# First-layer products beside attention values issued as four column tiles, with new instruction orders, in a fused attention and MLP kernel

## The chip, the cores and the metric

The kernel runs on one NeuronCore of a Trainium2 chip. The metric is the device time of one execution in microseconds, given as the median of three runs. A profiled execution is a separate run of the same program.

## The reference

Causal attention with 16 "beacon" keys in front, followed by an MLP with a GELU in its sigmoid form. Eight batches, eight heads, 576 positions, head size 64; the MLP takes 4,608 tokens from 512 to 2,048 features and back.

```python
k_all = np.concatenate([beacon_k, k], axis=2)
v_all = np.concatenate([beacon_v, v], axis=2)
scores = scale * np.matmul(q, k_all.transpose(0, 1, 3, 2))
scores = np.where(causal, -1000000000.0, scores)      # the beacons are never masked
a = np.exp(scores - scores.max(-1, keepdims=True))
a /= a.sum(-1, keepdims=True) + 1e-09
x = np.matmul(a, v_all)            # then (B, H, S, D) -> (B*S, H*D)
h = x @ w_in
g = h * (1.0 / (1.0 + np.exp(-1.702 * h)))
out = g @ w_out                    # float32, 4608 x 512
```

## The kernel before

The attention works on 16 sets; set s is batch s // 2 and four of the eight heads. Keys and queries are loaded and cast to 16 bit by DMAs that POOL issues (L362), turned by VectorE (`e_turn`, L418), and multiplied in chunks of at most 512 score columns for each head (`e_qk`, L447). There are 55 chunks, named here scores 0 to 54. A score product contracts over 32 rows, and the four heads stand in four row tiles of the array (32\*128). ScalarE takes the exponential (`e_exp`, L458) into a buffer E, POOL masks the blocks on the diagonal (`e_mask`, L479; for the first two sets VectorE masks some), and `e_av` (L534) multiplies by the values: for each head 32 columns of V, so that four heads stand in four column tiles (128\*32) and write four parts of one PSUM bank. The same operation with a matrix of ones gives the sums for the division; VectorE turns and inverts these (L546 to L557) and normalises the values into xT (`e_norm`, L569). From set 4 on (batch 2), the sum of a set comes from a tile zs that VectorE adds up (L497).

The MLP follows in ten groups of tokens, two of 256 and eight of 512. The first layer has 16 steps a group when the group is 512 tokens wide (`e_m1`, L593): each is four matmuls of 128\*128 over 512 columns into one PSUM bank. xT holds four batches, 2,304 tokens, as a ring; where a group wraps around its end, a step is eight matmuls of 256. In groups 0 and 1, ScalarE computes a tanh and VectorE finishes the gate (L607, L626); in groups 2 to 9 ScalarE computes the GELU itself (`e_gelu`, L614). The exponential and this GELU are in different tables of ScalarE, and each change is an ACT_TABLE_LOAD. The second layer is a plain product in groups 0 and 1 (`e_m2`, L638) and a Strassen-Winograd form in groups 2 to 9 (`e_prod`, L707, seven products of 128\*128 tiles over 256 columns, with sums of operands made by VectorE, L658, and results joined by VectorE, L723). Stores go out on SyncE's queue.

Values, first-layer steps and second-layer products share four PSUM banks (tiles u0 to u3, `RING = 4`); the scores have the other four as one buffer, so the next scores wait for the exponential of the last. A bank comes free when the operation that closes it has read it: the GELU for a first-layer step, normalisation or inversion for values, a join for a product.

Loads through POOL are followed on eight DMA lanes: a POOL load waits until the eighth load before it has landed, and whatever stands behind it in POOL's order waits too. POOL is an in-order queue of loads and masks.

The order of work on each engine is written out by hand as lists of operation numbers, `ORDER`, one for each of PE, ACT, DVE, POOL, Q (the landing of a load) and SP. `Plan.run` walks these lists, works out a start time for each operation from costs and latencies (`LAT`), chooses a PSUM bank for each step by these times, and emits the operations sorted by start. It therefore doesn't change the order on an engine. The plan charges 114 ns where PE's `mode` changes between "m" (128\*128), "r" (row tiles) and "c" (column tiles). Names of operations below: `m1.g.n` is step n of group g's first layer, `m2.g.p.n` a part of product p of group g (for groups 0 and 1: row block p, quarter n), `av s.x.h` the values (x = 0 or 1) or sums (x = 2) of set s in half h.

Of the kernel before, what the change touches and what calls it, by code (L numbers as in the profile page):

```python
# [17 lines left out]
        76, 100, 115, 118, 120, 106, 138, 141, 143, 108, 155, 111, 152, 129, 161, 158, 122, 131, 164, 167, 134, 127,  # L18
        170, 173, 176, 145, 125, 148, 150, 177, 182, 188, 191, 227, 194, 197, 232, 183, 203, 234, 200, 178, 237,
        179, 206, 258, 241, 209, 184, 263, 185, 212, 265, 213, 248, 246, 268, 214, 215, 401, 251, 253, 272, 218,  # L20
        404, 275, 244, 279, 219, 220, 407, 282, 284, 277, 221, 414, 320, 296, 304, 290, 302, 292, 300, 298, 312,
        308, 294, 318, 314, 310, 306, 316, 426, 435, 423, 343, 338, 339, 340, 433, 431, 438, 344, 345, 359, 349,
        341, 464, 346, 350, 351, 352, 354, 574, 355, 429, 360, 361, 577, 356, 362, 357, 372, 365, 583, 474, 477,
        373, 366, 374, 367, 605, 480, 484, 375, 482, 607, 368, 506, 502, 488, 492, 610, 490, 486, 498, 504, 500,
        508, 514, 510, 516, 494, 496, 512, 534, 593, 596, 535, 536, 539, 540, 550, 541, 542, 537, 742, 545, 546,
        547, 548, 603, 745, 551, 552, 553, 599, 601, 619, 622, 748, 555, 556, 557, 558, 561, 755, 625, 627, 629,
        562, 563, 776, 568, 564, 569, 570, 571, 779, 764, 767, 659, 637, 641, 657, 649, 651, 647, 661, 635, 631,
        653, 805, 772, 770, 774, 643, 655, 633, 639, 645, 679, 680, 815, 818, 700, 681, 682, 684, 701, 915, 690,
        685, 686, 691, 692, 702, 918, 687, 693, 695, 703, 696, 924, 821, 823, 697, 698, 706, 946, 825, 707, 713,
        708, 709, 948, 934, 937, 714, 715, 716, 827, 951, 944, 940, 942, 853, 831, 833, 855, 857, 851, 843, 835,  # L30
        837, 847, 839, 845, 829, 849, 841, 1083, 960, 963, 875, 876, 880, 877, 878, 881, 882, 1086, 968, 966, 970,
        883, 1089, 902, 909, 903, 886, 891, 1096, 887, 888, 889, 892, 893, 1117, 904, 894, 905, 896, 897, 1120, 898,
        899, 910, 911, 1105, 1108, 1146, 912, 976, 994, 996, 972, 978, 1000, 992, 982, 974, 998, 990, 984, 988, 980,
        1002, 986, 1256, 1156, 1113, 1111, 1115, 1159, 1025, 1020, 1026, 1021, 1259, 1022, 1027, 1031, 1023, 1028,
        1265, 1164, 1162, 1166, 1041, 1042, 1287, 1036, 1047, 1032, 1048, 1033, 1037, 1038, 1034, 1039, 1289, 1054,
        1055, 1049, 1056, 1043, 1044, 1050, 1292, 1057, 1198, 1172, 1168, 1178, 1184, 1180, 1194, 1170, 1174, 1176,
        1275, 1278, 1182, 1186, 1196, 1188, 1190, 1281, 1301, 1285, 1283, 1304, 1216, 1217, 1221, 1192, 1222, 1227,
        1218, 1223, 1228, 1219, 1224, 1232, 1229, 1233, 1230, 1307, 1311, 1309, 1237, 1327, 1333, 1238, 1243, 1234,
        1244, 1235, 1323, 1239, 1245, 1250, 1251, 1341, 1240, 1246, 1252, 1253, 1337, 1405, 1315, 1331, 1343, 1411,
        1335, 1321, 1403, 1431, 1313, 1325, 1407, 1419, 1317, 1423, 1425, 1319, 1339, 1421, 1409, 1329, 1361, 1413,  # L40
        1366, 1382, 1429, 1362, 1363, 1401, 1367, 1364, 1427, 1368, 1383, 1372, 1369, 1373, 1374, 1375, 1388, 1377,
        1389, 1378, 1390, 1395, 1379, 1384, 1380, 1385, 1391, 1396, 1415, 1397, 1398, 1470, 1454, 1417, 1455, 1449,
        1471, 1450, 1451, 1476, 1452, 1456, 1477, 1457, 1478, 1460, 1461, 1462, 1463, 1465, 1466, 1467, 1468, 1472,
        1479, 1473, 1483, 1484, 1485, 1486,
# [3 lines left out]
        195, 198, 233, 235, 201, 204, 238, 180, 207, 259, 210, 264, 186, 266, 269, 216, 402, 405, 408, 222, 417,  # L48
        415, 297, 291, 303, 305, 301, 299, 293, 309, 321, 295, 319, 313, 315, 311, 307, 317, 436, 439, 342, 465,
        468, 575, 578, 584, 587, 606, 608, 503, 507, 489, 491, 493, 487, 499, 505, 509, 515, 517, 495, 501, 511,  # L50
        497, 513, 611, 538, 743, 746, 749, 756, 758, 777, 780, 660, 642, 638, 652, 658, 648, 650, 636, 632, 662,
        654, 806, 644, 634, 656, 640, 646, 809, 916, 683, 919, 928, 925, 947, 949, 952, 828, 832, 854, 856, 852,
        858, 834, 838, 844, 840, 836, 846, 830, 848, 850, 842, 1084, 879, 1087, 1090, 1099, 1097, 1118, 1121, 1147,
        1150, 977, 995, 979, 997, 993, 973, 975, 983, 991, 999, 989, 1001, 981, 1003, 985, 987, 1257, 1260, 1024,
        1269, 1266, 1288, 1290, 1293, 1199, 1179, 1173, 1181, 1185, 1195, 1171, 1169, 1175, 1177, 1183, 1187, 1197,
        1189, 1191, 1193, 1220, 1328, 1334, 1324, 1342, 1316, 1332, 1344, 1406, 1412, 1338, 1336, 1404, 1432, 1314,
        1408, 1420, 1318, 1424, 1326, 1426, 1320, 1340, 1422, 1410, 1330, 1322, 1414, 1430, 1402, 1365, 1428, 1416,
        1418, 1453,
# [3 lines left out]
        123, 163, 160, 124, 224, 169, 128, 166, 172, 175, 146, 147, 126, 149, 151, 225, 226, 398, 190, 193, 196,  # L62
        199, 255, 256, 257, 202, 205, 286, 242, 411, 287, 211, 208, 243, 399, 249, 247, 400, 250, 412, 254, 252,
        273, 245, 274, 280, 276, 413, 281, 285, 283, 278, 289, 461, 288, 462, 419, 580, 420, 463, 326, 327, 328,
        421, 322, 92, 323, 324, 422, 427, 428, 424, 425, 325, 330, 334, 329, 335, 432, 336, 331, 434, 337, 332, 333,
        470, 347, 582, 353, 471, 581, 472, 430, 473, 358, 363, 475, 476, 478, 479, 481, 485, 739, 483, 369, 376,
        370, 589, 752, 740, 590, 615, 518, 753, 921, 519, 754, 526, 591, 527, 520, 528, 592, 529, 521, 741, 522,
        597, 523, 594, 530, 595, 598, 531, 802, 532, 524, 533, 616, 543, 525, 604, 549, 617, 618, 554, 600, 620,
        602, 623, 624, 621, 559, 760, 628, 761, 762, 626, 630, 565, 763, 566, 768, 572, 765, 811, 812, 766, 803,
        804, 769, 773, 771, 671, 1080, 775, 672, 813, 922, 663, 814, 664, 675, 667, 816, 673, 819, 668, 669, 817,  # L70
        923, 665, 666, 820, 674, 676, 677, 1093, 670, 688, 694, 678, 930, 822, 824, 699, 931, 826, 932, 933, 704,
        710, 938, 939, 935, 936, 717, 711, 945, 941, 943, 1081, 956, 957, 958, 871, 1082, 1094, 1095, 959, 872, 873,
        867, 859, 961, 962, 964, 965, 860, 863, 1262, 1143, 861, 874, 862, 868, 864, 967, 865, 971, 866, 969, 884,
        869, 870, 1101, 1144, 890, 1145, 1102, 895, 1103, 1104, 900, 906, 1109, 907, 1110, 913, 1106, 1107, 1152,
        1153, 1004, 1154, 1005, 1155, 1264, 1006, 1263, 1016, 1012, 1017, 1157, 1114, 1112, 1013, 1018, 1116, 1160,
        1008, 1161, 1009, 1019, 1158, 1014, 1015, 1029, 1010, 1165, 1011, 1007, 1163, 1167, 1035, 1040, 1271, 1051,
        1045, 1058, 1052, 1297, 1272, 1273, 1274, 1298, 1299, 1276, 1279, 1300, 1200, 1204, 1280, 1201, 1277, 1205,
        1282, 1302, 1206, 1286, 1284, 1208, 1305, 1209, 1202, 1303, 1210, 1212, 1203, 1306, 1207, 1213, 1225, 1231,
        1308, 1312, 1214, 1310, 1215, 1211, 1236, 1247, 1241, 1248, 1254, 1349, 1345, 1350, 1346, 1347, 1353, 1351,
        1354, 1355, 1356, 1357, 1358, 1359, 1370, 1348, 1360, 1352, 1376, 1381, 1386, 1392, 1393, 1445, 1446, 1433,  # L80
        1399, 1437, 1434, 1438, 1447, 1435, 1441, 1442, 1436, 1443, 1444, 1439, 1448, 1440, 1458, 1464, 1469, 1480,
        1474, 1481, 1487,
    ],
    "POOL": [
        8, 10, 12, 14, 16, 17, 19, 21, 23, 25, 27, 29, 31, 33, 35, 37, 39, 41, 43, 45, 47, 110, 49, 51, 113, 114,
        53, 55, 57, 59, 133, 61, 136, 137, 63, 65, 67, 69, 71, 378, 230, 231, 229, 380, 382, 384, 386, 236, 388,
# [29 lines left out]

class Plan:

    LANES = 8
    LAT = {"PE": 230, "ACT": 178, "DVE": 212, "POOL": 110, "Q": 1400, "SP": 0}

    def __init__(self, ring):
        self.ops = []
        self.ring = ring
        self.tiles = {}
        self.closers = {}
# [1004 lines left out]
```

## Time and profile before

| | |
|---|---|
| median of 3 runs | 329.88 us (329.2 to 330.05) |
| profiled execution | 328.92 us, span 327.2 us |
| granted TensorE clock, mean | 0.999 |
| TensorE (PE) busy | 314.6 us, 4,364 matmul records |
| VectorE (DVE) busy | 237.2 us |
| ScalarE (ACT) busy | 202.1 us |
| GpSimd (POOL) busy | 113.9 us |

| group of instructions | count | busy us | mean ns of one |
|---|---|---|---|
| L593 PE, first layer, 128 x 512 and 128 x 256 | 704 | 130.6 | 341 |
| L707 PE, second layer, 128 x 256 | 896 | 121.0 | 273 |
| L447 PE, scores, 20 shapes | 1376 | 34.6 | 228 |
| L534 PE, values from E and V | 928 | 27.4 | 262 |
| L614 ACT, GELU | 128 | 70.5 | 598 |
| L458 ACT, exponentials | 66 | 98.9 | 1515 |

The span runs from the first to the last instruction; the device time has what lies around it as well. Busy time is the union of an engine's instructions. Matmuls are pipelined: the length of one is longer than the distance to the next one, so rates are read from starts. Matmuls in different tiles of the array overlap, and four of them start within some 10 ns. "Idle before" and "<-" name the time an engine stood still ahead of a row, and what ended it.

### The profile page before, as it was taken

How to read it: one execution, taken by the hardware profiler on the slowest of the kernel's cores; microseconds unless marked ns; L12 is line 12 of the kernel's file. 1: busy time of each engine (PE TensorE's matmuls, PEld its weight loads, DVE VectorE, ACT ScalarE, POOL GpSimd, SP SyncE). 2: the span in 40 equal slices, each digit the busy share in tenths (PEclk: the TensorE clock that was granted, in tenths of full speed). 3: DMA queues.
4: the chain of work that ended last, by engine and by line, in shares of the span. 5: the costliest groups of instructions: out<-in, count | busy, mean ns of one | idle time of the engine just before them, and what ended most of it. 6: DMA issues, size and time to landing. Idle time of an engine off the chain costs nothing.

```text
span 327.2 us, 9966 instructions
## 1 busy us (share of the span) xinstructions
PE 314.6 (96%) x4364; PEld 214.7 (66%) x4364; DVE 237.2 (72%) x480; ACT 202.1 (62%) x236; POOL 113.9 (35%) x178
## 2 busy tenths in 40 slices
PE   6589999999999999999999999999999999999995
PEld 6467665545775477746878878547764776447884
DVE  4838798777987989977998798858558853006674
ACT  1676697678767586679666786868577212674010
POOL 8765478190419312941177019400042000000000
PEclk9999999999999999999999999999999999999999
DMA  7999999293424911792039709500120012000122
GB/s 126 159 201 211 204 186 184 37 123 107 99 72 64 190 34 34 79 198 43 7 53 178 119 4 124 154 2 3 34 98 0 2 34 83 15 0 2 65 98 97
DMA packets 58220, 28.83 MB, mean 88 GB/s; under 512 B 41280, under 2 KB 53568, under 8 KB 58176
## 3 DMA queue, kind: packets, MB, share of 16 engines
q0 software_dynamic: 47552, 18.49, 47.9%
q1 hardware_dynamic: 10560, 9.69, 9.2%
q8 instruction: 34, 0.56, 0.7%
q14 instruction: 10, 0.08, 0.1%
q10 hardware_dynamic: 64, 0.01, 0.0%
HBM read 37.22 MB, written 9.44 MB: 143 GB/s over the span
## 4 chain that ended last, share of the span: by engine, by line
PE 83%; DMA 6%; DVE 4%; POOL 3%; ACT 2%; issue 1%; ACTq 0%; POOLq 0%
PE u L593 34%; PE u L707 30%; PE u L534 9%; PE s L447 7%; PE u L638 3%; DMA w<-in_moe_w_out_dram 3%; DMA w<-in_moe_w_in_dram 3%; ACT E L458 1%; DVE sA L658 1%; DVE g L626 1%; POOL vb L378 1%; POOL w L384 0%; DVE bkn L403 0%; ACT L614 0%; DVE kT L418 0%
## 5 line engine op out<-in xcount | busy, mean ns | idle before, releaser
L593 PE MATMUL u<-xT,w 128*128 128x512 f16 (+1 forms) x704 | 130.6, 341 | 0.6 <-ACT g L614 0.5
L458 ACT ACTIVATE E<-s 128x2048 f16<-128x2048 f32 (+5 forms) x66 | 98.9, 1515 | 44.9 <-PE s L447 44.4
L614 ACT ACTIVATE g<-u 128x512 f16<-128x512 f32 x128 | 70.5, 598 | 53.7 <-PE u L593 53.2
L593 PEld LDWEIGHTS <-w 128*128 128x128 f16 x704 | 67.6, 98 | 54.3 <-issue 1.9
L479 POOL TENSOR_SCALAR_AFFINE_SELECT E<-E 128x512 f16<-128x512 f16 (+3 forms) x78 | 49.3, 665 | 110.8 <-ACT E L458 79.1
L723 DVE SCALAR_TENSOR_TENSOR osb<-u,osb 128x512 f32<-128x512 f32 x56 | 37.3, 683 | 24.5 <-PE u L707 22.5
L707 PEld LDWEIGHTS <-g 128*128 128x128 f16 x512 | 48.3, 98 | 9.3 <-issue 0.2
L707 PE MATMUL u<-w,g 128*128 128x256 f16 x384 | 50.6, 273 | 0.0
L447 PE MATMUL s<-qT,kT 32*128 32x32 f16 (+20 forms) x1376 | 34.6, 228 | 5.7 <-ACT E L458 2.8
L447 PEld LDWEIGHTS <-kT 32*128 32x128 f16 x1376 | 25.2, 92 | 22.5 <-issue 14.4
L707 PEld LDWEIGHTS <-sA 128*128 128x128 f16 x384 | 36.3, 98 | 5.3 <-issue 0.3
L707 PE MATMUL u<-tB,sA 128*128 128x256 f16 x256 | 35.1, 273 | 0.1
L658 DVE TENSOR_TENSOR sA<-g 128x512 f16<-128x512 f16 x32 | 12.9, 416 | 26.2 <-ACT g L614 26.2
L569 DVE TENSOR_TENSOR xT<-u,rz 128x352 f16<-128x352 f32 (+2 forms) x52 | 25.5, 517 | 6.5 <-PE u L534 6.3
L378 POOL DMA_DIRECT2D vb<-in_v_dram x32 | 27.4, 876 | 2.4 <-DMA qn<-in_q_dram 1.6
L534 PE MATMUL u<-E,vb 128*32 128x352 f16 (+8 forms) x928 | 27.4, 262 | 0.0
L497 DVE TENSOR_TENSOR zs<-zs,E 128x1344 f16<-128x1344 f16 (+2 forms) x36 | 22.7, 633 | 5.3 <-POOL E L479 4.4
L534 PEld LDWEIGHTS <-vb 128*32 128x32 f16 (+1 forms) x928 | 19.9, 96 | 5.5 <-issue 1.7
L418 DVE STREAM_TRANSPOSE kT<-kn 128x576 f32<-128x576 f32 x16 | 20.1, 1257 | 2.1 <-DMA kn<-in_k_dram 1.4
L418 DVE STREAM_TRANSPOSE qT<-qn 128x576 f32<-128x576 f32 x16 | 19.9, 1241 | 0.3 <-DMA qn<-in_q_dram 0.3
L546 DVE STREAM_TRANSPOSE zt<-u 128x224 f32<-128x224 f32 (+2 forms) x32 | 15.0, 470 | 5.9 <-PE u L534 5.8
L497 DVE TENSOR_TENSOR zs<-E 128x1856 f16<-128x1856 f16 x12 | 15.8, 1320 | 3.3 <-POOL E L479 3.3
(48 smaller groups left out, 252.3 us busy)
## 6 DMA issues: line engine op xcount, KB each, us to landing
out_dram<-osb SPq DMA_DIRECT2D x36, 256.0 KB, 2.4
kn<-in_k_dram POOLq DMA_DIRECT2D x16, 288.0 KB, 6.9
qn<-in_q_dram POOLq DMA_DIRECT2D x16, 288.0 KB, 6.5
vb<-in_v_dram POOLq DMA_DIRECT2D x24, 128.0 KB, 6.4
w<-in_moe_w_in_dram POOLq DMA_DIRECT2D x8, 256.0 KB, 9.4
w<-in_moe_w_out_dram POOLq DMA_DIRECT2D x4, 512.0 KB, 13.5
vb<-in_v_dram POOLq DMA_DIRECT2D x8, 112.0 KB, 5.0
vb<-in_v_dram POOLq DMA_DIRECT2D x8, 80.0 KB, 7.9
```

What stands on the lines that cost most here:

```text
L378: nc.gpsimd.dma_start(out=t[0 : hi - lo, j, h0:h1, :], in_=v[b, h0:h1, lo:hi, :].rearrange("h n d -> n h d"),)
L418: nc.vector.transpose(out=f32(dst.rearrange("p n e -> p (n e)")).rearrange("p (r t) -> p t r", t=TR), in_=f32(src[:, :]).rearrange("p (t c ...
L447: nc.tensor.matmul(sc[:, h, o : o + w], kT[s % NB2][r : r + 32, j * P : (j + 1) * P, d], qT[s % NB2][r : r + 32, a : a + w, d], start=(d = ...
L458: nc.scalar.activation(out=Es[s][:, :, c0:c1], in_=ss[i][:, :, o : o + c1 - c0], func=AFT.Exp, scale=0.125,)
L479: nc.gpsimd.affine_select(out=blk, in_=blk, compare_op=ALU.is_ge, fill=0.0, base=off + (Nb if j == 0 else 0), pattern=[[0, Q], [1, w]], ch ...
L497: nc.vector.tensor_tensor(out=t, in0=E[:, :, Z0:S] if i == 1 else t, in1=E[:, :, wcol[i] : wcol[i] + S - a], op=ALU.add,)
L534: nc.tensor.matmul(u[32 * h : 32 * h + 32, a:e], lhs, src[0:kw, h, col : col + e - a], start=first, stop=last,)
L569: nc.vector.tensor_tensor(out=xT[:, 2 * hs + x : 2 * hs + x + n, t0 : t0 + w], in0=rings[("av", s, x, half)][:, 0 : n * w].rearrange("p (n ...
L593: nc.tensor.matmul(u[:, o + a - t0 : o + e - t0], w1t[:, kp, nt * P : (nt + 1) * P], xT[:, kp, a % XR : (e - 1) % XR + 1], start=(kp == 0) ...
L614: nc.scalar.activation(out=gts[g][:, n0:n1, 0:w], in_=rings[("m1", g, n0)][:, 0 : n * w].rearrange("p (n w) -> p n w", n=n), func=AFT.Gelu ...
L707: nc.tensor.matmul(u[:, HM * mt : HM * (mt + 1)], lhs[:, n, mt * P : (mt + 1) * P], rhs[:, n, :], start=(n == 0 and mt == 0), stop=(n == H ...
L723: nc.vector.scalar_tensor_tensor(out=osbs[(g, dst)][:, :], in0=rings[("p", g, p)][:, :], scalar=scale_of(g), in1=osbs[(g, src)][:, :], op0 ...
```

## The change

Three things change. First, `Plan.tiled` goes through PE's list and cuts it into runs of one mode. A run of first-layer steps, with nothing else in it, that has values next to it on at least one side and holds at most 20 matmuls (five steps of a 512-token group) is issued as column tiles: each 128\*128 matmul becomes four of 128\*32 that write the four 32-partition parts of the same bank. The plan counts such steps as mode "c". 53 steps qualify in the new order.

Second, the plan's model of the output buffers: it gets a latency of 2,200 ns for a store, and each half or join that takes one of the four output buffers depends on the store that used the buffer last. Both are read by the plan only.

Third, the lists of `ORDER` are others from the last part of the first group on, on PE, ACT, DVE, POOL, Q and SP. The number and kind of operations stays as it was.

```diff
-    LAT = {"PE": 230, "ACT": 178, "DVE": 212, "POOL": 110, "Q": 1400, "SP": 0}
+    LAT = {"PE": 230, "ACT": 178, "DVE": 212, "POOL": 110, "Q": 1400, "SP": 2200}
...
+    def tiled(self):
+        runs = []
+        for i in ORDER["PE"]:
+            o = self.ops[i]
+            if not runs or runs[-1][0] != o.mode:
+                runs.append([o.mode, []])
+            runs[-1][1].append(o)
+        got = set()
+        for x, y, z in zip(runs, runs[1:], runs[2:]):
+            wide = all(o.name.startswith("m1.") and o.count == 4 for o in y[1])
+            if y[0] == "m" and wide and "c" in (x[0], z[0]) and sum(o.count for o in y[1]) <= 20:
+                got.update(o.seq for o in y[1])
+        return got
...
-                        m = o.mode
+                        m = "c" if o.seq in small else o.mode
...
                 for kp in range(NKT if a < e else 0):
-                    nc.tensor.matmul(
-                        u[:, o + a - t0 : o + e - t0],
-                        w1t[:, kp, nt * P : (nt + 1) * P],
-                        xT[:, kp, a % XR : (e - 1) % XR + 1],
-                        start=(kp == 0),
-                        stop=(kp == NKT - 1),
-                    )
+                    for r0, r1 in ((r, r + 32) for r in range(0, P, 32)) if tiled[0] else ((0, P),):
+                        nc.tensor.matmul(
+                            u[r0:r1, o + a - t0 : o + e - t0],
+                            w1t[:, kp, nt * P + r0 : nt * P + r1],
+                            xT[:, kp, a % XR : (e - 1) % XR + 1],
+                            start=(kp == 0),
+                            stop=(kp == NKT - 1),
+                        )
...
+        was = outs[-4:]
+
         def store(o, i, r, c):
-            op("SP", 60, [o], lambda: e_store4(g, i, r, c), name="store")
+            outs.append(op("SP", 60, [o], lambda: e_store4(g, i, r, c), name="store"))
...
-        half = op("ACT", 480, [last[1], ends.get(g - 1)], ...
+        half = op("ACT", 480, [last[1], ends.get(g - 1), was[0]], ...
...
+        outs[-4:] = outs[-1:] + [outs[-4], outs[-2], outs[-3]]
...
+    small = plan.tiled()
...
+        tiled[0] = o.seq in small
         o.emit()
```

Of the lists, the parts that matter here, with the numbers written out as names (v1.-1 is the load of the beacon rows of V for batch 1, v1.0 to v1.4 the blocks of 128 keys; q4 and k4 are loads for set 4):

```
POOL, from the last load of w_out on
before: w_out, mask 1, v1.-1, mask 1, mask 1, v1.0, v1.1, v1.2, v1.3, v1.4, k4, mask 2 x3, q4, k5, q5, v2.-1, mask 2, v2.0, ...
after:  w_out, q4, mask 1, mask 1, mask 1, v2.-1, v1.0, k4, v1.2, q5, mask 2 x2, v1.4, mask 2, v1.1, mask 2, v1.-1, k5,
        mask 2 x2, mask 3, v1.3, ...

PE, end of the first group
before: scores 7, av 0.1.1, m1.0.12, m1.0.14, m2.0.0.0, av 1.2.1, ...
after:  scores 7, m1.0.12, m1.0.14, m2.0.0.0, av 0.1.1, av 1.2.1, ...

PE, start of group 2
before: scores 18, av x3, m2.1.1.3, scores 19, m1.2.15, m1.2.9, m1.2.11, m1.2.0, m1.2.10, ...
after:  scores 18, av x2, m2.1.1.2, scores 19, m2.1.1.3, m1.2.0, m1.2.3, m1.2.1, m1.2.4, m1.2.11, ...
ACT there, before: evacuation, exponentials, GELU;  after: exponentials, evacuation, GELU

PE, scores 23 to 24
before: scores 23, m2.2.7.2, av 4.0.0, m2.2.4.2, m2.2.4.4, scores 24
after:  scores 23, m2.2.2.6, m2.2.7.4, m2.2.4.4, m2.2.6.6, av 4.0.0, scores 24

PE, group 4
before: scores 34, av 8.2.1, av 8.2.0, m1.4 x11, scores 35, av 8.0.1, av 8.0.0, av 8.1.1, m1.4 x5, m2.4 ...
after:  scores 34, m2.3.3.6, m1.4 x6, scores 35, m1.4, av 8.2.1, m1.4, av 8.2.0, m1.4 x5, av 8.0.0, m1.4 x3, av 8.1.1, ...
```

## The prediction

> **What bounds the kernel now.** I read the page first: span, busy times, slices, and the chain that ended last.
>
> ```profile
> span 327.2 us, 9966 instructions
> PE 314.6 (96%) x4364; PEld 214.7 (66%) x4364; DVE 237.2 (72%) x480; ACT 202.1 (62%) x236; POOL 113.9 (35%) x178
> PE   6589999999999999999999999999999999999995
> PE 83%; DMA 6%; DVE 4%; POOL 3%; ACT 2%; issue 1%; ACTq 0%; POOLq 0%
> ```
>
> TensorE (PE) is full from the fourth slice, about 31 us, to the end, and the chain runs along it. So from 31 us on, time changes only by what PE does per matmul, by what it loses between two array tilings, and by waits. The second view is PE's timeline around scores 35 (columns: start, length, engine, line, operation, count).
>
> ```profile
> 147.21 0.66 PE L447 MATMUL s<-qT,kT 32*128 32x256 f16 x32
> 147.79 1.61 PE L534 MATMUL u<-E,vb 128*32 128x352 f16 x56
> 149.34 4.49 PE L593 MATMUL u<-xT,w 128*128 128x512 f16 x20
> 153.66 1.04 PE L707 MATMUL u<-w,g 128*128 128x256 f16 x8
> 154.63 0.38 PE L534 MATMUL u<-zs,ones 128*32 128x352 f16 x8
> 154.84 0.23 PE L534 MATMUL u<-E,ones 128*32 128x80 f16 x8
> 155.00 0.61 PE L707 MATMUL u<-tB,g 128*128 128x256 f16 x4
> ```
>
> Starts give the rates; lengths overlap. First layer (L593) to second layer (L707), both 128*128: 153.66 − 149.34 = 4.32 us for twenty matmuls, 216 ns each, no loss at the seam. L707 to values (L534, 128*32): 154.63 − 153.66 = 0.97, but eight at 109 ns are 0.87, so 0.10 us is lost where the tiling changes. Back, 154.84 to 155.00: groups of 80 and 32 columns take 0.065, the other 0.095 is the change. Over the whole trace I took start-to-start times at each change, less the usual spacing; medians in ns: full to row tiles 96, row to full 99, row to column 97, column to row 109, full to column 93, column to full 107.
>
> The third view is ACT's timeline at two places, the start of group 2's first layer and the scores inside group 4's, with PE's rows for the first of them.
>
> ```profile
> 65.62 1.94 ACT L458 ACTIVATE E<-s 128x1536 f16<-128x1536 f32 x2
> 67.58 1.28 ACT L614 ACT_TABLE_LOAD   x1
> 68.87 1.08 ACT L614 ACTIVATE g<-u 128x512 f16<-128x512 f32 x2
> ```
>
> ```profile
> 65.40 3.63 PE L593 MATMUL u<-xT,w 128*128 128x512 f16 x16
> 69.52 1.67 PE L593 MATMUL u<-xT,w 128*128 128x512 f16 x7 [0.49 <-ACT g L614]
> ```
>
> ```profile
> 148.04 1.28 ACT L458 ACT_TABLE_LOAD   x1
> 149.33 1.02 ACT L458 ACTIVATE E<-s 128x1024 f16<-128x1024 f32 x1
> 150.38 1.28 ACT L614 ACT_TABLE_LOAD   x1
> 151.67 2.79 ACT L614 ACTIVATE g<-u 128x512 f16<-128x512 f32 x5
> ```
>
> An exponential between two GELUs costs ACT two table loads: from 148.02 to 151.67 it frees no PSUM bank, and PE has four. The fourth view is POOL's timeline in the head, and the value row that its masks release.
>
> ```profile
> 27.46 0.49 POOL L479 TENSOR_SCALAR_AFFINE_SELECT E<-E 128x320 f16<-128x320 f16 x1
> 29.27 0.54 POOL L367 DMA_DIRECT2D vb<-in_beacon_v_dram  x1 [1.32 <-DMA w<-in_moe_w_out_dram]
> 29.81 1.07 POOL L479 TENSOR_SCALAR_AFFINE_SELECT E<-E 128x512 f16<-128x512 f16 x2
> ```
>
> ```profile
> 30.16 0.99 PE L534 MATMUL u<-E,ones 128*32 128x288 f16 x20
> ```
>
> POOL's next load waits until an earlier load of w_out has landed; two masks stand behind it, and PE's last group of that row, due at 30.63, starts at 30.93.
>
> **Part 1, fewer tiling changes.** Counting PE's list in both kernels: 151 changes become 135. By kind: full to row +1, row to full +5, row to column −5, column to row −1, full to column −6, column to full −10. With the medians: 96 + 495 − 485 − 109 − 558 − 1070 = **−1.63 us**.
>
> **Part 2, the tiles themselves.** 53 first-layer steps become 260 groups of four (164 of 512 columns, 96 of 256): 780 more matmuls and 780 more weight loads. No row shows four column tiles at 512, so I bound it. The full tiles give a line: 109 ns at 256, 216 at 512, so 0.418 ns a column plus 2. Value groups are spaced 150 ns at 352 columns (line 149), 142 at 336 (142), 122.5 at 288 (122), 97.5 at 224 (96): 0 to 2 ns above. The 14 groups from 147.79 hold 3,328 columns; the line gives 1.42, the rows 1.55 less one change, 1.45: also 2 ns each. The far bound is the row tiles of L447, 218.5 ns at 480 against 203: 16 ns, 4.2 us in all. Below nothing is excluded: the same columns must stream. I take the value groups, the same tiling: 260 × 0.8 = **+0.2 us**.
>
> The Trainium skill, "TensorE: Matmul & The Clock Gate", section "Measured speedup vs the span model", speaks against this part: a pack of tiles lasts one matmul plus some 4 ns for each further tile. The trace shows that 3 to 4 ns between starts inside a group, but the next group starts on the line; if the 12 ns did add, the sum would be 3.1 us worse in place of 0.2, an estimate from that page.
>
> The weight loads: four of 32 columns take 97 ns each, one of 128 takes 98. Value groups of 80 columns stand 39 ns apart with four loads each, so the loads run side by side and hide; one after another they would need 388 ns of a 216 ns group. The Trainium skill, "TensorEngine Tiling", "Restrictions and Gotchas", says that column tiling excludes Fast Weight Load; here no load grew longer by it, so I add nothing.
>
> **Part 3, the new orders.** The entries that only the plan reads (the store latency, the output buffers' dependences) add no instruction; joins wait for no store in the waits view, and if one did, a store lands 2.4 us after its issue. Five places remain.
>
> Head: POOL now issues the load of q for set 4 where the beacon load stood, ahead of all three masks of set 1 and not after the first. It waits for the same landing, to 29.27. Then 0.56 issue, masks of 0.43, 0.59 and 0.48: the last ends at 31.32 and not 30.88. Moving one value row behind the w_out product does not help, since the last group waits for that mask: **+0.44**.
>
> Start of group 2: PE now keeps 0.86 us (a second-layer step) after the scores; ACT has its 0.50 evacuation behind the exponentials. PE needs 0.10 + 0.86 + 4 × 0.864 = 4.42 after the scores until it lacks a bank; ACT needs about 0.22 + 1.84 + 0.50 + 0.10 + 1.28 + 0.65 = 4.59. The wait, 0.66 in the rows (69.52 − 65.40 − 4 × 0.864), becomes 0.17: **−0.50**.
>
> Group 4: scores 35 now stand after six of the sixteen steps and no long run of values follows. Banks come back as in the rows: the last GELU ended 0.81 after the scores began, 3.65 of tables and exponential, 0.60 GELU, 0.05: 5.11. PE's work: 0.58 scores, four steps of 0.864, value rows of 0.15 and 0.11: 4.30. It waits about 0.8, of which I take **+0.75**; in the rows shown it waited for none, as 1.55 us of values came first.
>
> Gone: pauses of 0.15, 0.16 and 0.10 at the first full ring of groups 4, 6 and 7 (start-to-start over 216 ns at 140.7, 210.5, 244.2), since second-layer steps, scores or values now stand there: **−0.41**. Scores 24 waited 0.15 for an exponential (due 92.65, started 92.81); one more product stands before them: **−0.15**.
>
> Small: value rows now come up to five in a row, with four banks freed by 0.4 to 0.5 us normalisations; five or six places could wait 0.05 to 0.12 each: **+0.35**, with bounds 0 and 0.7. DVE is busy 62.4 of 71.0 us between 66 and 137, so it is there that such waits are likeliest.
>
> Sum: −1.63 + 0.2 + 0.44 − 0.50 + 0.75 − 0.41 − 0.15 + 0.35 = **−0.95 us**. The profiled execution took 328.92 (span 327.2 and 1.7 around it) and would take 327.97; it lies 0.96 under the median of the three runs, 329.88, so the forecast for that is 328.9. About 0.3% (1.0 us) is what a measurement of this kernel can tell from no change; the forecast lies at that edge.
>
> **Rivals.** (a) The new waits do not come, because the banks and masks are a little earlier than I walked: without +0.44, +0.75 and +0.35 the time is 327.4. For it: each is under a microsecond and rests on one execution's landing times. Against: the head's order is plain in the list.
>
> (b) Slower by the tiles: all four column tiles now stream the same columns of xT, where value tiles read four different ones. If that costs as row tiles do, 16 ns a group, the time is 332.9. It is slower than before beyond 4.5 ns a group (0.8 + 0.95 us over 260 groups), and by over 0.3% beyond 8 ns. For: row tiles grow with width. Against: the value groups lie on the line.
>
> (c) Slower by value loads of batch 1: two of them now stand behind masks of sets 2 and 3. The beacon rows would be issued about 45 and, at 7.7 us to landing in that stretch, land at 52.8; set 2's values want them at 53.4. The fourth block, issued about 49.5 behind a mask of set 3 and landing in 6.9, arrives at 56.4 for 56.9. With the 10.4 us of the stretch before, it is 3 us late: 331.9. By over 0.3% it decides from 1.9 us late. Against: fewer loads have been issued by then than before.
>
> (d) The drain stays between values and products, for a reason other than tiling: then Part 1 is nothing, and the time is 330.5. Against: L593 to L707 shows none.
>
> **How the numbers follow.** Forecast 0.55, split about evenly by the 0.3% edge (0.27 faster, 0.27 within, 0.01 slower); (a) 0.15, all faster; (b) 0.12, of it 0.07 slower; (c) 0.13, of it 0.09 slower; (d) 0.05, of it 0.02 slower. Faster 0.42, within 0.39, slower 0.19. The range takes in (a) below and the milder halves of (b) and (c) above: 327.4 to 331.0.
>
> **What would show it.** In the profile after: L593 in two forms, its column-tiled groups of 512 spaced 216 to 218 ns (Part 2 wrong beyond 220); no 0.1 us step between values and L593; POOL's first mask of set 1 at about 29.8 and the value row's last group near 31.4; PE idle before L593 small near 68 and 0.6 to 0.8 us near 146, released by ACT; no PE wait for a DMA near 53 or 57. PE's busy share should stay near 96%. The prediction is wrong if the end moves by over 2 us, or if PE waits anywhere past 60 us on DVE for more than half a microsecond.

## The result, and the profile after

The changed kernel takes 330.7 us (median of 21 runs, 329.4 to 332.2), the kernel before, on the same chips, 329.12 (21 runs): 1.0051 times as long, 95% interval 1.0037 to 1.0065. It is slower by 1.6 us, where the forecast was 1.0 faster. The forecast's 328.9 and its range of 327.4 to 331.0 were counted from 329.88, the median of three runs, which lies 0.76 above that of the 21. Counted from 329.12 the range would end at 330.2; that 330.7 lies inside it is luck.

Its profiled execution was the fastest of the 21 (329.4). From its page:

```profile
span 327.7 us, 11524 instructions
...
PE 315.8 (96%) x5144; PEld 221.4 (68%) x5144; DVE 238.5 (73%) x480; ACT 201.6 (62%) x236; POOL 114.5 (35%) x178
...
PE   7699999999999999999999999999999999999995
...
q8 instruction: 40, 0.66, 0.8%
```

PE is as full as before; the page alone would not tell the two kernels apart. The last line becomes important below: the DMA queue that brings instructions moved 40 packets, 34 in the kernel before. Since 329.4 is not typical, I profiled the same kernel again; that execution took 330.67, beside a median of 330.58 in its group, and the readings below are from it unless another is named. PE's waits past 30 us there (in all, how often, longest):

```profile
PE u L725 <- DVE g L676: 0.5, 1, 0.5
PE u L725 <- DVE osb L741: 0.5, 1, 0.5
PE u L611 <- ACT g L632: 0.4, 1, 0.4
PE s L462 <- issue: 0.4, 1, 0.4
PE u L725 <- DVE xT L584: 0.3, 1, 0.3
PE u L549 <- POOL E L494: 0.2, 1, 0.2
```

In the kernel before this view had one line past 31 us, the GELU's 0.5. L725 is the second layer (L707 before), L611 the first (L593), L676 the operand sums (L658), L741 the joins (L723), L512 the zs additions (L497), L494 the masks (L479), L462 the scores (L447). Three waits for VectorE are new, one for a mask, and one whose releaser is "issue": nothing that the profile shows.

I then took PE's starts past 31 us apart in both traces: the usual spacing, up to 100 ns at a tiling change, and what goes beyond as a wait.

| us | before (328.92) | after (330.67) | difference |
|---|---|---|---|
| start of the w_out product behind the head's value rows | 32.57 | 33.51 | +0.94 |
| tiling changes past 31 us | 12.43 (132) | 11.03 (117) | −1.40 |
| waits for VectorE | 0.52 | 1.62 | +1.10 |
| waits that no semaphore ends | 0 | 1.14 | +1.14 |
| waits for a GELU behind an exponential (groups 2 and 4) | 0.66 | 0.83 | +0.17 |
| other waits past 33 us | 0.80 | 0.59 | −0.21 |

These sum to +1.74; PE's last matmul starts 1.78 us later (323.11 and 324.88). Part of the first line is not the change's. The granted TensorE clock, here in tenths for 40 slices of the span, first before, then after, has a dip in the second slice:

```profile
PEclk9999999999999999999999999999999999999999
```

```profile
PEclk9899999999999999999999999999999999999999
```

From 14 to 17.5 us it was 1.00 in the profile of before, 0.50 in the first profile after and 0.56 in this one. The scores that start at 14.6 us here and in experiment 6, where the clock was 1.00, take 0.83 us here and 0.54 there. PE then came to the value row at 30.25 us; in experiments 7, 9 and 11, which have the same head and a clock of 1.00 there, it came at 29.71 to 29.89.

The column tiles themselves, in group 4:

```profile
144.10 1.05 PE L611 MATMUL u<-xT,w 128*32 128x512 f16 x16
144.97 0.32 PE L549 MATMUL u<-zs,ones 128*32 128x352 f16 x4
...
148.51 2.77 PE L611 MATMUL u<-xT,w 128*32 128x512 f16 x48 [0.45 <-ACT g L632]
```

```profile
144.23 1.28 ACT L473 ACT_TABLE_LOAD   x1
145.53 1.02 ACT L473 ACTIVATE E<-s 128x1024 f16<-128x1024 f32 x1
146.57 1.28 ACT L632 ACT_TABLE_LOAD   x1
147.86 2.06 ACT L632 ACTIVATE g<-u 128x512 f16<-128x512 f32 x4
```

Sixteen matmuls are four groups, and the values follow after 0.87 us: 217 ns a group and no loss at the seam. Behind the two table loads PE waits 0.63 for its bank. Both lie within what was predicted (216 to 218 ns, 0.6 to 0.8 us). What was not predicted is at 122 us. VectorE, POOL and PE:

```profile
121.94 0.83 DVE L676 TENSOR_TENSOR sA<-g,sA 128x512 f16<-128x512 f16 x1
122.70 1.28 DVE L512 TENSOR_TENSOR zs<-zs,E 128x1344 f16<-128x1344 f16 x1
123.90 0.68 DVE L676 TENSOR_TENSOR g<-g 128x512 f16<-128x512 f16 x1
```

```profile
121.19 0.63 POOL L494 TENSOR_SCALAR_AFFINE_SELECT E<-E 128x512 f16<-128x512 f16 x1 [5.36 <-ACT E L473]
121.77 0.58 POOL L377 DMA_DIRECT2D qn<-in_q_dram  x1
122.35 1.96 POOL L494 TENSOR_SCALAR_AFFINE_SELECT E<-E 128x512 f16<-128x512 f16 x2
```

```profile
124.64 0.61 PE L725 MATMUL u<-w,g 128*128 128x256 f16 x4 [0.51 <-DVE g L676]
```

An operand sum takes 0.42 us elsewhere; beside these masks two take 0.83 and 0.68, and a zs addition 1.28 where others of its size take 0.84. PE's second layer waits 0.67 for the last of the three (start to start; the view counts from the modelled end of the matmul before). At 164 us a sum takes 1.22 beside a mask and the beacon load, three normalisations stand behind it, and PE waits 0.40 for their bank; at 235 us a zs addition of 1.32 beside a mask, and a sum of 0.68 behind it, hold up a join, and PE waits 0.55:

```profile
164.29 1.22 DVE L676 TENSOR_TENSOR g<-g 128x512 f16<-128x512 f16 x1
164.57 0.65 POOL L494 TENSOR_SCALAR_AFFINE_SELECT E<-E 128x512 f16<-128x512 f16 x1
166.10 0.60 PE L725 MATMUL u<-tB,sA 128*128 128x256 f16 x4 [0.32 <-DVE xT L584]
...
233.60 1.32 DVE L512 TENSOR_TENSOR zs<-zs,E 128x1344 f16<-128x1344 f16 x1 [0.55 <-ACT E L473]
236.18 1.03 PE L725 MATMUL u<-w,g 128*128 128x256 f16 x8 [0.48 <-DVE osb L741]
```

The busy time of each engine from 117 to 130 us, before and after, shows what the new POOL list did there:

```profile
117.00:130.00 13.00, 13.00 (x224) 10.21 (x222) 12.32 (x30) 9.93 (x8) 2.75 (x4) 1.00 0.06 22
```

```profile
117.00:130.00 13.00, 12.49 (x217) 9.32 (x216) 12.09 (x28) 9.26 (x8) 5.23 (x7) 1.00 0.51 65
```

Columns are PE, weight loads, DVE, ACT, POOL, clock, DMA share, GB/s. VectorE has 0.7 to 0.9 us to spare in 13 in both, and POOL works 5.23 us beside it in place of 2.75.

### The profile page after: what moved, and what is told of

It is laid out like the page before. It is cut to its first block, busy times and chain, and to the rows that moved or that the text cites. A ratio compares the mean times of both kernels' runs of the same rounds, so it can differ in the third digit from the quotient of the medians.

```text
span 327.7 us, 11524 instructions
## 1 busy us (share of the span) xinstructions
PE 315.8 (96%) x5144; PEld 221.4 (68%) x5144; DVE 238.5 (73%) x480; ACT 201.6 (62%) x236; POOL 114.5 (35%) x178
## 5 line engine op out<-in xcount | busy, mean ns | idle before, releaser
L611 PE MATMUL u<-xT,w 128*32 128x512 f16 (+3 forms) x1484 | 133.5, 341 | 0.7 <-ACT g L632 0.5
L611 PEld LDWEIGHTS <-w 128*32 128x32 f16 (+1 forms) x1484 | 71.7, 97 | 49.9 <-issue 2.1
L494 POOL TENSOR_SCALAR_AFFINE_SELECT E<-E 128x512 f16<-128x512 f16 (+3 forms) x78 | 50.1, 660 | 61.8 <-ACT E L473 56.6
L725 PEld LDWEIGHTS <-g 128*128 128x128 f16 x512 | 48.4, 98 | 8.7 <-DVE g L676 0.8
L741 DVE SCALAR_TENSOR_TENSOR osb<-u,osb 128x512 f32<-128x512 f32 x56 | 37.5, 686 | 19.6 <-PE u L725 11.8
L725 PE MATMUL u<-w,g 128*128 128x256 f16 x384 | 50.3, 273 | 1.0 <-DVE g L676 0.5
L725 PEld LDWEIGHTS <-sA 128*128 128x128 f16 x384 | 36.7, 98 | 5.5 <-issue 0.5
L462 PEld LDWEIGHTS <-kT 32*128 32x128 f16 x1376 | 25.7, 94 | 21.5 <-issue 13.8
L462 PE MATMUL s<-qT,kT 32*128 32x32 f16 (+20 forms) x1376 | 35.2, 232 | 4.1 <-DVE qT L433 2.3
L676 DVE TENSOR_TENSOR sA<-g 128x512 f16<-128x512 f16 x32 | 13.4, 417 | 34.5 <-ACT g L632 34.4
L725 PE MATMUL u<-tB,sA 128*128 128x256 f16 x256 | 36.4, 273 | 0.3 <-DVE xT L584 0.3
L549 PE MATMUL u<-E,vb 128*32 128x352 f16 (+8 forms) x928 | 28.7, 265 | 0.0
L549 PEld LDWEIGHTS <-vb 128*32 128x32 f16 (+1 forms) x928 | 21.6, 97 | 6.3 <-issue 1.3
L512 DVE TENSOR_TENSOR zs<-zs,E 128x1344 f16<-128x1344 f16 (+2 forms) x36 | 22.5, 631 | 3.3 <-POOL E L494 2.2
L561 DVE STREAM_TRANSPOSE zt<-u 128x352 f32<-128x352 f32 (+2 forms) x32 | 14.8, 473 | 8.5 <-PE u L549 8.2
L725 PE MATMUL u<-w,sA 128*128 128x256 f16 x128 | 17.9, 273 | 0.0
```

What stands on the lines that cost most here:

```text
L462: nc.tensor.matmul(sc[:, h, o : o + w], kT[s % NB2][r : r + 32, j * P : (j + 1) * P, d], qT[s % NB2][r : r + 32, a : a + w, d], start=(d = ...
L494: nc.gpsimd.affine_select(out=blk, in_=blk, compare_op=ALU.is_ge, fill=0.0, base=off + (Nb if j == 0 else 0), pattern=[[0, Q], [1, w]], ch ...
L512: nc.vector.tensor_tensor(out=t, in0=E[:, :, Z0:S] if i == 1 else t, in1=E[:, :, wcol[i] : wcol[i] + S - a], op=ALU.add,)
L549: nc.tensor.matmul(u[32 * h : 32 * h + 32, a:e], lhs, src[0:kw, h, col : col + e - a], start=first, stop=last,)
L611: nc.tensor.matmul(u[r0:r1, o + a - t0 : o + e - t0], w1t[:, kp, nt * P + r0 : nt * P + r1], xT[:, kp, a % XR : (e - 1) % XR + 1], start=( ...
L725: nc.tensor.matmul(u[:, HM * mt : HM * (mt + 1)], lhs[:, n, mt * P : (mt + 1) * P], rhs[:, n, :], start=(n == 0 and mt == 0), stop=(n == H ...
```

## The experiments

Letters name the theories of an expectation; the same letter can stand for another theory in another experiment.

**1. The new orders without column tiles.**

```diff
-    small = plan.tiled()
+    small = set()
```

> The new orders with every first-layer matmul as one full tile; the tiles alone are undone. TensorE's list then changes tiling 171 times, 36 more than the changed kernel (full to column +19, column to full +17, row to full +3, the rest -3), 3.6 us by the medians of the rows. Theory A (the tiles are free and save what the switches cost; the loss is in the orders): 3.0 to 3.8 us above the changed kernel, about 5 us above the kernel before. Theory B (the tiles cost time that the trace does not show, some 10 ns a group or more): less than 1.5 us above the changed kernel.

Measured: 332.48 us, ratio to before 1.0106 (1.0087 to 1.0125). By the ratios the tiles are worth 1.8 to 2.1 us, less than theory A expected and more than B. By the medians 36 changes are 3.6 us; group 4's wait falls from 0.63 to 0.26 here, and the waits without a semaphore (1.14) are absent, so 1.5 of the 3.6 are given back once the steps are tiled. The new lists are built for tiles: without them they have 171 changes.

**2. The old lists with the tiling rule.** The changed kernel with the former ORDER.

> The orders of before with all the rest of the change. Only one run of first-layer steps qualifies there, so tiling changes go from 151 to 149. Theory A (orders): 0.2 us faster than before, not to be told from no change. Theory B (tiles): the same, since 20 groups alone are tiled, at most 0.2 us slower. If it is slower by 1 us or more, the code around the orders (bank choice, plan latencies) is at fault.

Measured: 328.97, ratio 0.9998 (0.9988 to 1.0007). Only two changes go; the rule brings nothing by itself, and costs nothing.

**3 and 4. Masks of eight columns, in both kernels.**

```diff
+            blk = blk[:, :, 0:8]
...
-                pattern=[[0, Q], [1, w]],
+                pattern=[[0, Q], [1, 8]],
```

> The changed kernel with each of POOL's masks cut to its first 8 columns; the rest of the mask is left out, so POOL's mask work shrinks from 50 us to a few, and the dependences stay. Theory A1 (VectorE's operand sums and results are late because POOL's masks hold them up, and the new orders leave them no slack): the waits of TensorE for VectorE at 123, 165, 183 and 235 us go, and the time falls by 1.5 to 2.5 us, more than in the kernel before with the same cut. Theory A2 (the new orders lose at the group 4 exponential and in the loads, POOL's masks have no part in it): falls by the same as the kernel before does, within 0.4 us.

> The control to the run before: the kernel before with each of POOL's masks cut to its first 8 columns, the rest of the mask left out. Theory A1: falls by only 0.3 to 0.8 us (one wait of 0.28 us at 86 us and the head), so that the changed kernel with narrow masks is the faster of the two, by about 1 us. Theory A2: the distance between the two kernels stays at 1.6 us.

Measured: the changed kernel falls to 328.76 (0.999, 0.9975 to 1.0004), by 1.9; the kernel before to 328.60 (0.9985, 0.9975 to 0.9995), by 0.5. PE's waits past 40 us with short masks are these two:

```profile
PE u L612 <- issue: 0.7, 1, 0.7
PE u L612 <- ACT g L633: 0.4, 1, 0.4
```

All waits for VectorE in this view are gone (lines are one number higher in this kernel), and no operand sum takes over 0.43 us. So POOL's masks are what lengthens VectorE here. But the changed kernel does not come out ahead of the other, as its fewer tiling changes should make it, and an "issue" wait stands there.

**5. Three moves on VectorE.**

```diff
-  528, 616, 529,                    # in VectorE's list: 616 zs addition, 529 operand sum
+  528, 529, 616,
...
-  678, 822, 826, 824,               # 678 operand sum, the others normalisations
+  822, 826, 824, 678,
...
-  1272, 1015, 1029, 1035, 1019,     # 1272 zs addition, 1029 and 1035 joins
+  1015, 1029, 1035, 1019, 1272,
```

> The changed kernel with three moves in VectorE's list: one operand sum ahead of the zs addition it stood behind, one operand sum behind the three normalisations that stood behind it, and one zs addition behind two joins and a sum. Nothing else differs. A (operand sums and zs additions, lengthened beside GpSimd's work, hold back what frees a bank): PE's waits of 0.68 us at 122.8, 0.40 at 164.5 and 0.55 at 234.2 fall under 0.15 each, and the time is 1.2 to 1.6 us under the changed kernel's 330.7, so 329.1 to 329.5. B (these waits only show slack that PE would lose anyway a little later; the loss comes from the head and group 4): new waits of like size follow within 10 us, and the time stays at 330.2 to 331.0.

Measured: 331.1 (1.0068, 1.0051 to 1.0086), not faster. The three waits are gone, and others have come:

```profile
PE u L611 <- issue: 1.2, 1, 1.2
PE u L611 <- ACT g L632: 0.4, 1, 0.4
PE u L611 <- DVE osb L741: 0.4, 1, 0.4
PE u L549 <- issue: 0.3, 1, 0.3
PE s L462 <- issue: 0.3, 1, 0.3
```

For the wait near 123, PE waits 0.26 and 0.28 near 127; for that near 165, 0.22 and 0.52 near 174, where four joins stand in a row. Only the wait near 235 went without a successor. A falls as put: two of the three moves only chose who waits. The "issue" waits are 2.27 us here and 1.14 in experiment 8; as two executions of the changed kernel have 0.36 and 1.14, the moves need not be what raised them.

**6. The masks of set 1 ahead of the load of q.**

```diff
-  380, 133, 136, 137, 386,          # in POOL's list: 380 load of q for set 4, 133, 136, 137 masks of set 1
+  133, 136, 137, 380, 386,
```

> The changed kernel with one move in GpSimd's list: the load of q for set 4 goes behind the three masks of set 1. By the prediction's head term PE's value row near 30 us gets its last group 0.44 us sooner, so the time is 0.3 to 0.5 us under the changed kernel's 330.7. A (the loss is VectorE's waits past 60 us, 2.0 us, and the head's 0.44 comes on top): 330.2 to 330.4. C (in a median run the load's wait for a landing is longer than in the profiled one, which is why the median lies 1.3 us over the profiled time): 329.2 to 329.7, and the runs lie closer together. D (a later wait takes the 0.44 back): 330.6 to 330.8.

Measured: 330.06 (1.0036, 1.0019 to 1.0054), between A and C. Its interval overlaps that of the changed kernel beside it (1.0042, 1.0030 to 1.0054), so the time alone is inconclusive. The trace says more: the value row waits for no mask, 0.66 us in experiment 8, and the w_out product starts at 32.40 and not 33.51. The other 0.45 of these 1.11 us is not the move's: PE came to the row at 29.80 and not 30.25, and the clock from 14 to 17.5 us was 1.00 and not 0.56. The "issue" wait near 182 is 0.9 here and not 0.3.

**7. Group 5 without column tiles.**

```diff
-    small = plan.tiled()
+    small = plan.tiled() - {o.seq for o in plan.ops if o.name.startswith("m1.5.")}
```

> The changed kernel with the twelve column-tiled steps of group 5, which are of 256 columns, as full tiles again: seven more tiling changes (142 for 135), 0.70 us by the medians. F (near 181 us PE runs out of instructions: after the first matmul of a step nothing follows for 0.36 us in the changed kernel's profile and 0.94 in the one with narrow masks, with no wait on a semaphore in between, while column tiles of 256 columns take eight instructions each 109 ns): the gap after a first matmul is gone, and the time is within 0.4 us of the changed kernel's 330.7. G (a bank that is late, not seen): the gap stays and the time is 331.2 to 331.6.

Measured: 330.55 (1.0048, 1.0029 to 1.0066): level with the changed kernel though it has seven more changes, and without the gap near 182. F, as far as the time goes. The gap near 60 us, where nothing is tiled by the change, was 1.13 in this profile.

**8. The changed kernel again.**

> The changed kernel once more, beside the others on one chip: 330.7 us expected, between 1.0037 and 1.0065 of the kernel before. If its profiled execution lies near the median this time: A expects the waits on VectorE at 122.8, 164.5 and 234.2 again, 2.0 us in all with the one near 181; C expects the value row near 31 us and the w_out product behind it later than the 31.46 and 33.05 us of the first profile, by about a microsecond.

Measured: 330.58 (1.0042, 1.0030 to 1.0054). The waits for VectorE come back to within 0.02 us; the w_out product is 0.46 later than in the first profile, not a microsecond, and the waits without a semaphore are 1.14 in place of 0.36.

What these look like, first in column tiles near 181 us (kernel of experiment 6), then in the scores near 60 (experiment 8):

```profile
180.02 1.14 PE L611 MATMUL u<-xT,w 128*32 128x256 f16 x33
181.92 2.35 PE L611 MATMUL u<-xT,w 128*32 128x256 f16 x77 [0.75 <-issue]
```

```profile
59.20 0.60 PE L462 MATMUL s<-qT,kT 32*128 32x448 f16 x10
60.21 0.23 PE L462 MATMUL s<-qT,kT 32*128 32x64 f16 x6 [0.41 <-issue]
```

Thirty-two matmuls are one step; the thirty-third begins the next, so its bank was free, and then not even a weight load follows for a microsecond. The instruction after the gap has no wait in the trace. The packet records of the instruction queue give the rest: PE's 10,301 recorded instructions came in 40 packets of 16 KB, one for 257 (8,743 in 34 before), and after each such gap, in seven profiles, PE goes on 2.2 to 2.6 us after the start of the latest packet. These gaps stand at four places of PE's list only, behind 1,985, 6,081, 6,337 or 6,593 recorded instructions. The places are whole multiples of 256 apart, and the packet just started is then the 7th, 23rd, 24th or 25th, in the same distances: PE stands where one packet's instructions end and the next one's begin. The later the packet, the longer the gap: near 60 us it is 0, 0.44, 0.57 and 1.13 for packets that start at 56.4, 57.5, 57.8 and 58.0.

**9 and 10. Value loads of batches 2 to 7 cut to one head, in both kernels.**

```diff
         t = vb[b % NB2]
+        h1 = h1 if b < 2 else h0 + 1
```

> The changed kernel with the value loads of batches 2 to 7 cut to the first head (one eighth of their bytes; the other heads keep what an earlier batch left). The profiles show four gaps of PE that no semaphore releases, in scores near 60 us (0 to 1.13 us), in column tiles near 182 (0.3 to 1.4) and near 188 (0 to 0.5), and PE goes on 2.2 to 2.4 us after the start of a 16 KB instruction transfer each time. F (these transfers come late because they stand behind value loads in the DMA engines): the gaps fall under 0.2, and the time is 0.8 to 1.3 us under the changed kernel's 330.6, so 329.3 to 329.8. G (column tiles use up instructions faster than they can come, whatever the loads): the gaps near 182 and 188 stay and the time is 330.2 to 330.7.

> The kernel before with the same cut of the value loads of batches 2 to 7 to one head. It shows no such gap. F and G: 328.7 to 329.1 against 329.0. If it gains like the changed kernel (0.8 or more), the loads cost something else, GpSimd's issues beside VectorE for one, and the comparison says nothing of the gaps.

Measured: the changed kernel 329.27 (1.0011, 1.0000 to 1.0022), down by 1.3; the kernel before 328.94 (0.9993, 0.9984 to 1.0002), down by 0.1. The gaps near 60 and 182 are gone, that near 189 stays at 0.3, so F's "under 0.2" holds for two of the three. The two are 0.87 us in the trace of experiment 8; another 0.43 of the distance between the traces lies in the head, where PE came to the value row at 29.81 and not 30.25. G falls for these two gaps: PE does not starve there by itself, it starves when a packet comes late, and with fewer bytes of loads the packet near 60 us starts at 55.3 and not 57.8, that is 1.8 us and not 3.85 after PE has begun on the instructions of the packet before.

**11. Three loads later, all bytes kept.**

```diff
-  390, 260, 271, 270, 267,          # in POOL's list: 390 value load, the others masks of set 3
+  260, 271, 270, 267, 390,
...
-  1127, 953, 929, 1072, 955, 1139, 1133,    # 1127 load of k, 1072, 1139, 1133 value loads, the others masks
+  953, 929, 955, 1139, 1133, 1127, 1072,
...
```

The list Q, the order of landings, follows the two late loads.

> The changed kernel with three loads later in GpSimd's list, all bytes kept: a value load of batch 2 goes from 52.5 us behind the next four masks, 5 us later, and a k load of set 15 and a value load of batch 6, issued at 176 and 178 us, go behind the next two value loads, to about 201. F: the instruction transfers near 58 and 180 us start 0.5 to 1.5 us sooner, the gap near 60 is under 0.2 and that near 182 under 0.2; 0.5 to 1.0 under the changed kernel's 330.6, so 329.6 to 330.1. G: no change, 330.4 to 330.8.

Measured: 329.93 (1.0024, 1.0012 to 1.0035), down by 0.65, as F said. The place of the former gap near 60 us:

```profile
58.85 0.64 PE L462 MATMUL s<-qT,kT 32*128 32x448 f16 x16
59.41 0.90 PE L549 MATMUL u<-E,vb 128*32 128x288 f16 x32
```

All sixteen score matmuls stand together, and the packets start at 56.1 and 178.5, not at 57.8 and 180.6. All three gaps are gone, and a wait of 0.77 us for an operand sum has come at 204 us.

**12. The later loads, the head's masks first, and one zs addition behind the joins:** the edits of 6 and 11 and the last of 5.

> The changed kernel with the later loads, the masks of set 1 ahead of the load of q, and one zs addition behind two joins and a sum on VectorE (the one of the three moves whose wait, 0.55 at 235, no later wait took the place of). If the gains add (head 0.5, join 0.5, instructions 0.5 to 1.0): 328.6 to 329.1, level with the kernel before. If they are taken back downstream as two of VectorE's moves were: 329.8 to 330.3.

Measured: 328.74 (0.9993, 0.9984 to 1.0003): the gains add, 1.8 us in all, and the change is level with the kernel before. The wait that experiment 11 brought shows in VectorE's rows and PE's:

```profile
201.37 1.53 DVE L512 TENSOR_TENSOR zs<-E 128x1856 f16<-128x1856 f16 x1 [1.57 <-POOL E L494]
202.83 0.79 DVE L676 TENSOR_TENSOR g<-g 128x512 f16<-128x512 f16 x1
```

```profile
203.68 0.61 PE L725 MATMUL u<-w,g 128*128 128x256 f16 x4 [0.60 <-DVE g L676]
```

The two moved loads stand ahead of three masks; VectorE is idle 1.57 us for them, and an operand sum that PE needs stands behind.

**13. The same two loads behind these masks.**

```diff
-  1139, 1133, 1127, 1072, 1088, 1091, 1085,
+  1139, 1133, 1088, 1091, 1085, 1127, 1072,
```

> The kernel with the three moves, but the two late loads (k of set 15, a value load of batch 6) go behind the next three masks of set 12 and not ahead of them. In the profile of the three moves these masks came 1.5 us later, VectorE's zs addition at 201.4 us waited for them, an operand sum stood behind it, and PE waited 0.77 us at 203. If that wait belongs to the place of the loads alone, it is under 0.1 and the time is 0.5 to 0.8 us under the 328.74 of the three moves: 327.9 to 328.3, faster than the kernel before (329.1) by 0.8 to 1.1 us. If VectorE has no slack there, as near 123 and 165 us, a like wait follows within 10 us: 328.5 to 328.9.

Measured: 328.29 (0.9979, 0.9969 to 0.9990), faster than the kernel before and 2.3 us below the changed kernel. Its span and all waits of PE past 40 us that the view lists:

```profile
span 326.1 us, 11522 instructions
```

```profile
PE u L725 <- DVE g L676: 0.5, 1, 0.5
PE u L611 <- ACT g L632: 0.4, 1, 0.4
PE u L725 <- DVE xT L584: 0.3, 1, 0.3
```

The wait near 203 is gone and no other came: there VectorE had slack. The step from experiment 12 is 0.45, a little under the 0.5 to 0.8 expected, and the two intervals still overlap a little; the trace is what shows the wait gone.

## Why the prediction was wrong

**Part 1 held.** Tiling changes past 31 us cost 1.40 us less (132 to 117); forecast 1.63 for all sixteen.

**Part 2 held as array time.** It forecast +0.2, and nothing is to be seen: groups stand 216 to 217 ns apart at 512 columns and 109 at 256. Rival (b) did not come, nor (d): the steps between values and L611 are gone. What the part left out is that 1,560 more instructions must also be brought: the forecast counted them and priced them only on the array. That missing term is part of the 1.14 us of gaps without a semaphore. Of these 0.57 near 60 us is not the tiles' own: it is scores and value rows, and a load list that makes the packet late. The prediction's rival (c) looked at those same loads and asked only when their own data lands; PE waits for no value near 53 or 57 us, but for its instructions behind them.

**Part 3, head, held.** It forecast +0.44. Where the head is the changed one and the clock was full (experiments 7, 9 and 11), the w_out product starts at 32.97, 33.08 and 33.16 us, 0.40 to 0.59 behind the 32.57 of before, and the value row waits 0.65 us for masks, where it waited 0.30 before. The changed kernel's own two profiles, +0.48 and +0.94, mix this with the dip of the clock. In the first, PE came to the value row at 30.45 and waited for no mask, so that +0.48 meets the forecast by luck. In the second it came at 30.25, and as the load of q was released at 29.78 (29.14 in the first), the masks behind it were late as well and PE waited 0.66:

```profile
29.78 0.54 POOL L377 DMA_DIRECT2D qn<-in_q_dram  x1 [2.10 <-DMA w<-in_moe_w_out_dram]
30.33 1.49 POOL L494 TENSOR_SCALAR_AFFINE_SELECT E<-E 128x320 f16<-128x320 f16 x3
```

```profile
31.45 0.64 PE L549 MATMUL u<-E,ones 128*32 128x208 f16 x8 [0.15 <-POOL E L494]
```

**Part 3, groups 2 and 4:** the wait near 69 us fell from 0.66 to 0.19 or 0.20 (forecast 0.17), that near 147 is 0.63 (0.75 forecast), released by ACT. The pauses of groups 6 and 7 are gone and that of group 4 is 0.08.

**Part 3, "Small", failed by what it left out.** It gave +0.35, bounds 0 and 0.7, for places where value rows wait for banks that VectorE frees. Such waits came at the size it gave to each, before value rows and column tiles: 0.06, 0.08 and 0.06 us at 53.7, 128.1 and 147.0, released by VectorE. What it put at nothing, without a reason, is that the second layer waits for VectorE as well: 0.67 for an operand sum at 124.6 us, 0.40 for a bank behind three normalisations at 166.1, 0.55 for a join at 236.2. That is 1.62 us, 1.10 more than VectorE cost PE before. Only the first of the three lies between 66 and 137 us, where the prediction thought such waits likeliest; the sign that would refute it, a wait on VectorE over half a microsecond, it named rightly. It took VectorE's durations from the rows of before, as if they were fixed. They hang on what POOL does at that moment (with short masks, experiment 3, the three waits are gone), and POOL's list was new. The prediction walked POOL's order only for loads and for the masks that PE waits for, not for what it does to VectorE.

Term by term the forecast's −0.95 and the trace's +1.74 lie 2.69 us apart: 1.14 for the instructions, 0.75 for the waits on VectorE beyond Small's 0.35, 0.50 for the head, where the dip of the clock in this execution put PE some 0.4 us late, and 0.30 net from the rest (Part 1 came out 0.23 smaller, the small pauses 0.35 less, Part 2 and the GELU's waits 0.28 better). Experiment 13, with the same tiles, is 0.6 us under the kernel before (328.9 beside it). In its profile, whose span is 1.1 us shorter, tiling changes cost 1.4 less, waits 0.6 more, and the w_out product starts 0.15 sooner: the fewer tiling changes were a real gain. It had been lost to where five operations stand on POOL and VectorE.

Open: that the packets stand in a queue behind the loads is inferred from experiments 9 and 11, since the trace shows when a packet starts and not when it was asked for; and experiment 9 also shortens POOL's issues, which experiment 10 bounds at 0.1 us only for the other lists.

## What to carry to other kernels

When a schedule is changed, walk each moved operation of POOL against VectorE's two-input 16-bit operations, and where a mask lies beside one, start the later of the two when the earlier ends: the sums here then took 0.67 to 1.23 us in place of 0.42. When one instruction is split into four, count the instructions per microsecond in the densest stretch and look at the "issue" waits, and keep bulk loads away from it. Here two waits that were taken away by reordering a nearly full VectorE came back 3 to 11 us later, and one that lay where it had slack did not, so look at the engine's idle time first.

## What the hardware showed that I had not expected

Operand sums (16-bit, 512 columns, two inputs) over six profiles (before, after, experiments 8, 11, 12 and 13): 418 ns at the median when POOL does nothing beside them (654 sums, none over 427), 410 beside DMA issues alone (43, three of them at 680 and no other over 463), 419 beside masks alone (41, up to 856), and 832 beside a mask and an issue (30, from 673 to 1,227). With masks of eight columns, in experiment 3, none takes over 427, so the masks have the main part in it. The Trainium skill, "SBUF — State Buffer", section "Who interferes with whom", says that a VectorE instruction with two inputs in SBUF contends with a GpSimd instruction that reads SBUF, and not with one that only writes; the rows agree on who is lengthened, apart from the three sums.

In its "Summary: rules for kernel authors" the page also says that of two such instructions the second one to issue is fully blocked until the first finishes. The rows agree. If a sum stands still for a mask and then takes its usual 0.42 us, its start follows from its end. For 34 of the 46 sums over 0.5 us in these profiles this start lies 0.12 to 0.15 us before the recorded end of a mask: the sum at 164 us ends at 165.51, so it ran from 165.09, and the mask's record ends at 165.22. It holds the other way round as well: for each of the 78 masks past 60 us that took over 0.1 us more than usual, it lies 0.11 to 0.17 us before the recorded end of a two-input operation of VectorE. At 122 us, where both sides are long (the zs addition 1.28 for 0.84, the two masks of 512 and 320 columns together 1.96 for 0.63 and 0.47), each thus waited in turn for the other. Of the other twelve sums, eight, the first at 122 us among them, end 0.42 us after a DMA issue ends, three stand beside an issue alone, and one fits neither; why these are long is open.

PE's instructions come by DMA in 16 KB packets, one for some 257 of them, and PE stood 0.2 to 1.4 us without instructions where such a packet started late beside bulk loads. PE was busy again 2.2 to 2.6 us after the start. Column tiles of 256 columns, eight instructions each 109 ns, use a packet in 3.5 us.
